# Query projection of the second layer in groups of four token tiles instead of two

## The chip, the core and the metric

One NeuronCore of a Trainium2 chip runs the whole program. The metric is the device time of one execution in microseconds (us). Its engines work side by side and wait for one another through semaphores: TensorE (PE; its weight loads are PEld), VectorE (DVE), ScalarE (ACT), GpSimd (POOL), and SyncE (SP), which here issues nearly all DMAs.

## The reference

Two kinds of layer alternate, twice each: A, B, A, B over 2048 tokens of width 576, with 32 heads of 18 channels.

```python
x = x + _A_ref(_layernorm(x), A_wq, A_wk, A_wv, A_wo)   # softmax attention, one key and value head
x = x + _B_ref(_layernorm(x), B_wqkv, B_w_phi, B_wo)    # linear attention on learned features
x = x + _A_ref(_layernorm(x), A_wq, A_wk, A_wv, A_wo)
x = x + _B_ref(_layernorm(x), B_wqkv, B_w_phi, B_wo)

def _A_ref(x, wq, wk, wv, wo):
    q = (x @ wq), split in 32 heads; k = x @ wk; v = x @ wv
    p = softmax(q k^T * 18 ** -0.5)
    return (p v, heads side by side) @ wo
```

What the change touches is `x @ wq`, `x @ wk` and `x @ wv` of the second A layer.

## The kernel before, in words

The program's "layer 0" is the first A and B pair, "layer 1" the second. Tokens lie in 16 tiles of 128. Each layer is (1) a setting up, which normalises every tile, turns it so that channels lie on partitions, and projects queries, keys and values; (2) a long attention part, in which ScalarE's exponentials and TensorE's score and value products alternate, with layer B's keys woven in; (3) a tail. The tail of layer 0's B layer and the setting up of layer 1 are one stretch: `token_tile` reads a tile's features back (`read_out`, L829), projects them with `wob` (L259), adds the residual (L324), and hands the tile on to `next_queries`.

**Ticks.** `pipelined` starts one tile per tick and moves every tile that is under way by one stage; jobs in `late` come at the end of the tick. So a tick of this stretch holds, from different tiles: the transposes of a normalised tile (`xn`, L310 and L314), the 28 products with `wob` on 288 columns, the transposes of a read-out (`xo`), and a read-out's 44 small products.

**Blocks.** After every second tile `next_queries` appends `project_queries` to `late`. Its core is 70 products, written together, which this text calls a block: five row tiles m (m = 4 first, which holds the last queries and the keys and values; its weights are `w4`), each the sum of 14 products over 256 columns (L467): four channel slots as high times high, high times low, low times high, and two products for the rest. The numbers are fp32 stored as an fp32r high part and the difference. For each m, ScalarE copies the bank to a piece `pc` (L492), VectorE makes the low part (L499) and a bf16 square (L501), and SP writes both parts to `qd` (L503). For m = 4 six further DMAs write the keys (L509), issued by SP, and by GpSimd for the last pair. After a STAGE, the next tick turns the values (L519), sums the squares over each head with `sel` (L523), and VectorE takes the maximum and a root (L524 to L529).

**Buffers.** The turned tokens lie in `xsc`, nine slots by 256 columns, with two buffers that alternate between pairs. `pc` has seven buffers. `featk` and `featq` are single buffers that lend `project_queries` its room. The seven banks of PSUM are handed out in turn.

**Order.** Instructions stand on each engine in the order that the scheduler gave them, and each engine runs in that order. `early` works beside the tiles: after four tiles it sets a level (`set_level`; L543 rewrites all of `kst`), after eight it loads the first queries and starts three score units.

Of the kernel before, what the change touches and what calls it, by code (L numbers as in the profile page):

```python
# [19 lines left out]
P = 128  # L20
S = 2048
D = 576
H = 32
DH = 18
NT = S // P
KT = 5
# [8 lines left out]
PAIR = 2  # L35
PW = PAIR * P
LEVEL = 4
KEYS = 3 * DH
STK = KEYS + 2
ROWT = 64  # L40
# [2 lines left out]
VROW = 64  # L43
# [19 lines left out]
def kernel(ctx, tc, x_in, wq, wk, wv, wo, wqkv, w_phi, wob, out):  # L63
    nc = tc.nc
# [242 lines left out]
    def transposed(xn, xs, ps, hi_engine, lo_engine=V):  # L307
        pa = ps.tile([P, 4, P], F32, name="ps")
        for k in range(4):
            T.transpose(pa[:, k, :], xn[:, k * P : (k + 1) * P], idf)  # L310
        split(xs[:, 0:4, :], xs[:, 5:9, :], pa, hi_engine, lo_engine)
        yield -440
        pb = ps.tile([P, P], F32, name="ps")
        T.transpose(pb, xn[:, 512:], idf)  # L314
        if hi_engine is A:
            A.activation(xs[:, 4, :], pb, AF.Copy)
        else:
            V.tensor_copy(xs[:, 4, :], pb)
        lo_engine.tensor_sub(xs[64:P, 4, :], pb[64:P, :], xs[64:P, 4, :].bitcast(F32))
        yield -110  # L320
# [127 lines left out]
    def clear_shifts():  # L448
        with tc.tile_pool(name="zero", bufs=1) as zp:
            z = zp.tile([P, 512], F32, name="z")  # L450
            V.memset(z, 0.0)
            for m in mxds:
                nc.sync.dma_start(m[1].rearrange("b c -> (b c)").rearrange("(p n) -> p n", p=P), z)

    def project_queries(p, layer, w, xsc, bw, pool, ps, norms):
        qd = qds[layer]
        keys = slice(p * PW, (p + 1) * PW)
        work = [bw.tile([P, H, 2, DH], F32, name=tag).rearrange("p h s d -> p (h s d)")
                for tag in ("featk", "featq")]
        sq = work[0][:, : KT * PW // 2].bitcast(BF16).rearrange("p (m t) -> p m t", t=PW)  # L460
        vt = work[0][:, KT * PW // 2 : KT * PW // 2 + PW]
        root = work[1][:H, :PW]

        def product(po, m, n):
            slot, half, k = PRODUCTS[n]
            lhs = w[half][:, k, m * P : (m + 1) * P] if m < 4 else w4[half][:, k, :]
            T.matmul(po, lhs, xsc[:, slot, :], start=(n == 0), stop=(n == LASTP))  # L467

        begun = {}
        opening = layer == 0 and p == 0  # L470
        if opening:
            for m in range(KT - 1):
                begun[m] = ps.tile([P, PW], F32, name="ps")
            mark = len(traced(nc))
            for n in range(len(PRODUCTS)):
                if n == TURN:
                    st["turn"]()
                for m in range(KT - 1):
                    product(begun[m], m, n)
        written_from = len(traced(nc))  # L480
        for m in (*range(KT - 1), KT - 1) if opening else (KT - 1, *range(KT - 1)):
            if layer == 0 and p == 1 and m == THIRD:
                st["turn third"]()
            po = begun.get(m)
            if po is None:
                po = ps.tile([P, PW], F32, name="ps")
                for n in range(len(PRODUCTS)):
                    product(po, m, n)
                if opening:
                    st["opening"] = traced(nc)[mark:]  # L490
            pc = pool.tile([P, 2, PW], F32R, name="pc", bufs=7)
            A.activation(pc[:, 0, :], po, AF.Copy)  # L492
            if m == 4:
                A.activation(vt, po, AF.Copy)
            top = pc[:, 0, :].bitcast(F32)
            squared = layer == 0 or p == NT // PAIR - 1
            if squared:
                A.activation(sq[:, m, :], po, AF.Square)
            V.tensor_sub(pc[:, 1, :], po, top)  # L499
            if not squared:  # L500
                V.tensor_mul(sq[:, m, :], top, top)  # L501
            rows = P if m < 4 else 64
            nc.sync.dma_start(qd[:, m * P : m * P + rows, keys].rearrange("j p t -> p j t"), pc[:rows].bitcast(F32))  # L503
            if m == KT - 1:
                queue = nc.gpsimd if p == NT // PAIR - 1 else nc.sync
                for j, piece in enumerate(KPIECES):
                    for base in (0, ROWT):
                        row = base + j * DH
                        queue.dma_start(kst[row : row + DH, keys].bitcast(F32),  # L509
                                          pc[KROW : KROW + DH, piece, :].bitcast(F32))  # L510
        if opening:
            st["third"]()
        elif layer == 0 and p <= 2:
            st["pinned"].extend(traced(nc)[written_from:])
        yield STAGE
        st["ready"] += PAIR
        pv = ps.tile([P, PAIR, P], F32, name="ps")
        for tt in range(PAIR):
            T.transpose(pv[:, tt, :], vt[:, tt * P : (tt + 1) * P], idf)  # L519
        V.tensor_copy(vst[:, p * PAIR : (p + 1) * PAIR, :DH], pv[:, :, VROW : VROW + DH])  # L520
        pn = ps.tile([P, PW], F32, name="ps")
        for m in range(KT):
            T.matmul(pn, sel[:, m, :], sq[:, m, :], start=(m == 0), stop=(m == KT - 1))  # L523
        V.tensor_reduce(norms[: H + 1, p : p + 1], pn[: H + 1], axis=AX.X, op=ALU.max)  # L524
        V.tensor_scalar(root.bitcast(I32), pn[:H].bitcast(I32), 1, None, op0=ALU.logical_shift_right)
        V.tensor_scalar(root.bitcast(I32), root.bitcast(I32), 1.0, float(0x1FC00000),
                        op0=ALU.mult, op1=ALU.add)
        length = pool.tile([P, PW], F32R, name="length", bufs=1)[:H]
        V.tensor_scalar(length, root, 1.02, None, op0=ALU.mult)  # L529
        nc.sync.dma_start(mxds[layer][0, :, keys], length.bitcast(F32))  # L530

# [314 lines left out]
            yield from project(po, st["wob"], b * HALF, xs, lambda: add_residual(i, b, po))  # L846

    def next_queries(i, stats, layer, st, xpool, sp, ps):
        p, tt = divmod(i, PAIR)
        xn = layer_norm(i, stats or ln_stats([i]), xpool, A)  # L850
        yield STAGE
        if tt == 0:
            st["xsc"] = sp.tile([P, 9, PW], F32R, name="xsc")
        xsc = st["xsc"]
        yield from transposed(xn, xsc[:, :, tt * P : (tt + 1) * P], ps, A)
        yield STAGE
        if tt == PAIR - 1:
            st["late"].append(project_queries(p, layer, st["wq"], xsc, bw, st["pieces"], ps, st["norms"]))

    def pipelined(jobs, late=(), fill=iter(())):  # L860
        jobs, active = deque(jobs), []
# [49 lines left out]
    def early(layer, st, ps):  # L911
        while st["ready"] < LEVEL:
            yield
        yield from set_level(st["norms"][:, : LEVEL // PAIR], st["limit"][layer], ps)
        while st["ready"] < BEGIN:
            yield
        for place in "ca"[: 1 if layer else 2]:
            st["head"] += room_spots(place)
            st["roomed"] += place
        load_queries(st["q0"], layer, 0, 0)  # L920
        load_shifts(st["q0"], layer, 0, 0)
        yield
        yield
        q1 = bw.tile([P, 9 * P], F32R, name="xs")
        st["q1"] = q1[:, : 2 * CW].rearrange("p (h t) -> p h t", t=CW)
        for n, pt in enumerate(st["head"]):
# [54 lines left out]
    def attend(layer, st, a1o, stream):  # L981
# [14 lines left out]
        with ctx1:  # L996
# [88 lines left out]
            last = {}  # L1085
# [47 lines left out]

            mark[0] = len(traced(nc))
            safe = []
            head(False, lambda: safe.append(decide_shift(st["norms"], st["limit"][layer], Spare())))
            in_order()
            last.clear()
            safe = safe[0]
# [181 lines left out]
    def settle(layer, ps, jobs):  # L1321
        st.update(ready=0, head=[], roomed="", begun=0)
        run(pipelined(jobs, st["late"], early(layer, st, ps)))
        st["slot"] = (ps.turn - 1) % 7 // 2 + 1

    with first, ExitStack() as ps:
        sp = s0
        st["pieces"] = s0q
        stats = {}

        def first_tile(i):
# [77 lines left out]
    for layer in range(LAYERS):  # L1409
# [196 lines left out]
        with psx, tc.tile_pool(name=f"s{layer + 1}", bufs=2) as sp, tc.tile_pool(name=f"s{layer + 1}q", bufs=1) as spq:  # L1606
            st["pieces"] = spq
            if not last:
                reload_w4(sp)

            def leave():
# [7 lines left out]
                both = sp.tile([P, 9, PW], F32R, name="xsc").bitcast(F32).rearrange("p a b -> p (a b)")  # L1619
                ek, eq = (both[:, k * 2 * D : (k + 1) * 2 * D].rearrange("p (h s d) -> p h s d", s=2, d=DH)  # L1620
                          for k in range(2))
# [88 lines left out]
```

## Time and profile before

| | us |
|---|---|
| median of three runs (2607.29, 2612.37, 2608.31) | 2608.31 |
| the profiled execution's own time | 2609.11 |
| its span, first to last instruction | 2607.2 |
| TensorE busy | 2576.6 |
| ScalarE busy | 2161.3 |
| VectorE busy | 1243.6 |
| setting up of layer 1, from its first block to its last products | 1253 to 1403 |

Times within the execution count from the start of the span. Busy time of TensorE is drawn from starts and modelled ends, and products overlap; so the price of a product is read from the distance between two starts of the timeline, not from its mean duration. The granted clock is 1.00 of full speed in every stretch used below.

### The profile page before, as it was taken

The page shows a single profiled execution, that of the slowest core. Times are in us where ns is not written, and L with a number is a line of the kernel's source. Part 1 is how long each engine was busy: PE and PEld are TensorE (multiplying, and loading weights), DVE is VectorE, ACT ScalarE, POOL GpSimd, SP SyncE. Part 2 cuts the span into 40 slices and gives each one's busy share as a digit, 9 for nine tenths or more (in the row PEclk, how much of TensorE's full clock was granted, in tenths as well). Part 3 has the DMA queues.
Part 4 walks back from the last instruction along what each step waited for, and adds up shares of the span by engine and source line. Part 5 has one row for each costly group of instructions (what it writes and reads, how often), then busy time and mean ns, then how long its engine had stood idle before and what let it go on. Part 6 is the DMA issues. An engine that isn't in the chain of part 4 may idle for free. (4 is left out here: it accounts for less than half of the span.)

```text
span 2607.2 us, 55668 instructions
## 1 busy us (share of the span) xinstructions
PE 2576.6 (99%) x22002; PEld 1429.5 (55%) x22002; DVE 1243.6 (48%) x2826; ACT 2161.3 (83%) x2583; POOL 89.0 (3%) x183
## 2 busy tenths in 40 slices
PE   8999999999999999999999999999999999999999
PEld 7634444444444444439996344444444444444598
DVE  7435554444444444427774424444444444444265
ACT  6699999999999999993336999999999999999721
POOL 1000000000000000002000000000000000000010
PEclk9999999999999999999999999999999999999999
DMA  6475442222222222226644312222222222222164
GB/s 201 142 179 146 120 138 61 60 54 56 58 60 57 58 58 61 61 53 189 200 129 148 80 44 61 61 59 56 61 57 61 61 61 61 61 61 59 35 200 144
DMA packets 491246, 232.96 MB, mean 89 GB/s; under 512 B 237902, under 2 KB 458166, under 8 KB 490978
## 3 DMA queue, kind: packets, MB, share of 16 engines
q1 hardware_dynamic: 490002, 227.04, 33.0%
q8 instruction: 176, 2.88, 0.5%
q0 software_dynamic: 976, 2.29, 0.3%
q14 instruction: 92, 0.75, 0.1%
HBM read 130.62 MB, written 96.67 MB: 87 GB/s over the span
## 5 line engine op out<-in xcount | busy, mean ns | idle before, releaser
L1103 ACT ACTIVATE pt<-sc 128x1024 f32<-128x1024 f32 x2032 | 1923.6, 1062 | 135.9 <-PE sc L598 114.9
L598 PE MATMUL sc<-qst,kst 56*128 56x512 f32 x3840 | 687.5, 450 | 1.5 <-ACT pt L1103 1.4
L598 PEld LDWEIGHTS sc<-qst,kst 56*128 56x128 f32 x3840 | 317.1, 184 | 555.3 <-ACT pt L1103 507.9
L878 PE MATMUL acc<-pt,vst 128*32 128x512 f32 x4096 | 510.7, 600 | 0.2 <-DVE vb L663 0.2
L878 PE MATMUL ps<-pt,vst 128*32 128x512 f32 x4048 | 481.3, 598 | 0.0
L878 PEld LDWEIGHTS ps<-pt,vst 128*32 128x32 f32 x4048 | 108.6, 109 | 224.4 <-issue 223.0
L878 PEld LDWEIGHTS acc<-pt,vst 128*32 128x32 f32 x4096 | 98.5, 108 | 200.7 <-issue 189.5
L324 DVE TENSOR_TENSOR xc<-xc,acc 128x288 f32<-128x288 f32 x59 | 26.8, 454 | 329.7 <-PE acc L259 329.7
L632 DVE COPY featq<-ps 128x288 f32<-128x288 f32 x52 | 23.8, 458 | 268.2 <-PE ps L259 268.2
L259 PE MATMUL ps<-wahi,xs 128*128 128x288 f32 x684 | 146.9, 301 | 0.6 <-ACT xs L133 0.6
L259 PE MATMUL ps<-wchi,xs 128*128 128x288 f32 x576 | 127.4, 306 | 0.0
L259 PE MATMUL acc<-wdhi,on 128*128 128x288 f32 x531 | 117.5, 306 | 0.0
L259 PEld LDWEIGHTS ps<-wahi,xs 128*128 128x128 f32 x684 | 111.8, 188 | 3.6 <-issue 1.7
L259 PE MATMUL ps<-walo,xs 128*128 128x288 f32 x380 | 111.3, 296 | 0.0
L467 PE MATMUL ps<-xsc,wbhi 128*128 128x256 f32 x576 | 109.1, 287 | 0.7 <-ACT xsc L133 0.6
L259 PE MATMUL acc<-wahi,xs 128*128 128x288 f32 x468 | 103.7, 307 | 2.4 <-DVE turned L1011 1.3
L291 POOL TENSOR_TENSOR rstd<-var,neghalf 128x1 f32<-128x1 f32 (+1 forms) x56 | 32.3, 576 | 2159.4 <-DVE mv L289 2142.2
L133 ACT ACTIVATE xs<-ps 128x512 fp32r<-128x512 f32 x36 | 21.4, 595 | 100.1 <-PE ps L310 100.1
L259 PEld LDWEIGHTS ps<-wchi,xs 128*128 128x128 f32 x576 | 94.1, 188 | 16.1 <-issue 15.8
L259 PEld LDWEIGHTS acc<-wdhi,on 128*128 128x128 f32 x531 | 86.5, 187 | 21.2 <-issue 21.2
L632 DVE COPY featk<-acc 128x288 f32<-128x288 f32 x52 | 23.8, 457 | 153.0 <-PE acc L259 153.0
L259 PE MATMUL ps<-wclo,xs 128*128 128x288 f32 x320 | 94.1, 294 | 0.0
(266 smaller groups left out, 3154.6 us busy)
## 6 DMA issues: line engine op xcount, KB each, us to landing
qst<-qd SPq DMA_DIRECT2D x360, 72.0 KB
od<-parts SPq DMA_DIRECT2D x512, 36.0 KB
pht<-phi SPq DMA_DIRECT2D x32, 540.0 KB
qd<-pc SPq DMA_DIRECT2D x64, 256.0 KB
on<-od SPq DMA_DIRECT2D x60, 256.0 KB
phi<-pht SPq DMA_DIRECT2D x104, 144.0 KB
xd<-xc SPq DMA_DIRECT2D x33, 288.0 KB
flipped<-pht SPq DMA_DIRECT2D x112, 72.0 KB
```

The source lines that it names most:

```text
L133: A.activation(dst_hi, src, AF.Copy)
L259: T.matmul(dst, xs[:, slot, :], w[half][:, k, c0 : c0 + HALF], start=(n == 0), stop=(n == last))
L291: G.tensor_tensor(rstd, var, neghalf[:, :n], op=ALU.pow)
L324: V.tensor_add(xr, xr, po)
L467: T.matmul(po, lhs, xsc[:, slot, :], start=(n == 0), stop=(n == LASTP))
L598: T.matmul(sc, kst[head_rows(h), t * P : (t + 1) * P], q[head_rows(h), h // 2, :], start=True, stop=True)
L632: V.tensor_copy(e[:, hs, 0, :], src)
L878: T.matmul(acc[32 * j : 32 * j + 32, :], vst[:, t, :], pts[j], start=first, stop=last)
L1103: A.activation(pt, sc, AF.Exp, scale=SCALE)
```

## The change

`GROUPS` gives each layer its groups of tiles: layer 0 keeps eight pairs, layer 1 has three groups of four and two pairs. A group of four is projected on 512 columns, one whole bank. The pieces `pc` of layer 1 become twice as wide and four instead of seven. `xsc` is one tile with two halves of two token tiles, in both layers; a group of four reads both halves at once. Of the group's room, the last square, the value rows and the root move to `featq`; the length is made in place. Layer 1's tail takes two `pc` buffers where it took one `xsc`.

```diff
+GROUPS = ((2,) * 8, (4, 4, 4, 2, 2))
+PIECES = (7, 4)
+    def piece_room(pool, layer):
+        widest = max(GROUPS[layer]) * P
+        return pool.tile([P, max(2 * widest, H * 2 * DH) if layer else 2 * widest], F32R, name="pc", bufs=PIECES[layer])
     def project_queries(p, layer, w, xsc, bw, pool, ps, norms):
-        keys = slice(p * PW, (p + 1) * PW)
+        size = GROUPS[layer][p]
+        width = size * P
+        begin = sum(GROUPS[layer][:p])
+        keys = slice(begin * P, (begin + size) * P)
+        tokens = xsc if size > PAIR else xsc[:, begin // PAIR % 2]
...
-            T.matmul(po, lhs, xsc[:, slot, :], start=(n == 0), stop=(n == LASTP))
+            moving = tokens[:, :, slot, :] if size > PAIR else tokens[:, slot, :]
+            T.matmul(po, lhs, moving, start=(n == 0), stop=(n == LASTP))
...
-                po = ps.tile([P, PW], F32, name="ps")
+                po = ps.tile([P, width], F32, name="ps")
...
-            pc = pool.tile([P, 2, PW], F32R, name="pc", bufs=7)
+            pc = piece_room(pool, layer)[:, : 2 * width].rearrange("p (j t) -> p j t", t=width)
...
     def next_queries(i, stats, layer, st, xpool, sp, ps):
-        p, tt = divmod(i, PAIR)
+        half, tt = i // PAIR % 2, i % PAIR
...
-        if tt == 0:
-            st["xsc"] = sp.tile([P, 9, PW], F32R, name="xsc")
...
-        yield from transposed(xn, xsc[:, :, tt * P : (tt + 1) * P], ps, A)
+        yield from transposed(xn, xsc[:, half, :, tt * P : (tt + 1) * P], ps, A)
...
-        if tt == PAIR - 1:
-            st["late"].append(project_queries(p, layer, st["wq"], xsc, bw, st["pieces"], ps, st["norms"]))
+        ends = [sum(GROUPS[layer][: p + 1]) - 1 for p in range(len(GROUPS[layer]))]
+        if i in ends:
+            st["late"].append(project_queries(ends.index(i), layer, st["wq"], xsc, bw, st["pieces"], ps, st["norms"]))
...
+    def token_room(pool):
+        return pool.tile([P, 2, 9, PW], F32R, name="xsc", bufs=1)
```

On all engines the instructions stand as before up to this stretch and after it; only names and widths differ. TensorE, where the first block stood before: behind the read-out of a tile came the first products on 256 columns (`w_14169` and `w_14170` are the two halves of `w4`, `kvb` and `pht` the read-out's operands).

```order
L310 MATMUL ps<-idf,xo 128x128 x4
L314 MATMUL ps<-idf,xo 128x128
L829 MATMUL ps<-kvb,pht 64x57 x20
L829 MATMUL ps<-kvb,pht 64x38 x2
L467 MATMUL ps<-xsc,w_14169 128x256
L467 MATMUL ps<-xsc,w_14170 128x256
```

In the changed kernel the same place on TensorE goes on with a further tile's transposes and its 28 products with `wob`.

```order
L312 MATMUL ps<-idf,xo 128x128 x4
L316 MATMUL ps<-idf,xo 128x128
L848 MATMUL ps<-kvb,pht 64x57 x20
L848 MATMUL ps<-kvb,pht 64x38 x2
L312 MATMUL ps<-idf,xn 128x128 x4
L316 MATMUL ps<-idf,xn 128x128
L261 MATMUL ps<-wahi,xs_15051 128x288
L261 MATMUL ps<-walo,xs_15051 128x288
```

The block has moved behind three more such ticks, to where the second pair's block stood, and holds both pairs; between the first and the second block, and between the second and the third, stand four ticks without one. Tile 4's transposes, too, stand ahead of the first block (tile 8's ahead of the second, tile 12's ahead of the third): they fill the quarter of `xsc` that the group's own first tile had, so that the products take the later tile's tokens there.

VectorE, one tick behind a pair's block, before: the values' copy, maximum and root (L520 to L529) among the steps of two other tiles.

```order
L520 COPY vst<-ps 128x2x18
L839 COPY xo<-xo 128x64
L524 TENSOR_REDUCE norms<-ps 33x1
L525 TENSOR_SCALAR featq<-ps 32x256
L136 TENSOR_TENSOR xsc<-ps,xsc 128x4x128
L526 TENSOR_SCALAR featq<-featq 32x256
L319 TENSOR_TENSOR xsc<-ps,xsc 64x128
L529 TENSOR_SCALAR length<-featq 32x256
L288 TENSOR_SCALAR var_15360<-mv_15355 128x1
```

VectorE at the same place behind the first group of four, after.

```order
L538 COPY vst<-ps 128x4x18
L858 COPY xo<-xo 128x64
L544 TENSOR_REDUCE norms<-ps 33x1
L545 TENSOR_SCALAR featq<-ps 32x512
L553 TENSOR_REDUCE top<-norms 33x1
L138 TENSOR_TENSOR xsc<-ps,xsc 128x4x128
L546 TENSOR_SCALAR featq<-featq 32x512
L321 TENSOR_TENSOR xsc<-ps,xsc 64x128
L548 TENSOR_SCALAR featq<-featq 32x512
L290 TENSOR_SCALAR var_15686<-mv_15681 128x1
```

The same steps stand there twice as wide, with `top` among them. Two further ticks without a block follow, where one did behind the first pair and none behind the others. VectorE two ticks later, after, where the level is written: `kst` (2048 columns) stands between the steps of two tiles.

```order
L579 TENSOR_TENSOR level<-ps,krows 128x1
L138 TENSOR_TENSOR xsc<-ps,xsc 128x4x128
L858 COPY xo<-xo 128x64
L562 TENSOR_SCALAR kst<-kst,krows,level 128x2048
L321 TENSOR_TENSOR xsc<-ps,xsc 64x128
L290 TENSOR_SCALAR var_15916<-mv_15911 128x1
```

Before, `kst` stood in the tick behind the third pair's norms, one tick ahead of a block; now it stands in the last tick ahead of the second block.

## Rows read from the trace of the kernel before

**Rows 1.** The page: busy time by engine, then the chain that ended last, by engine.

```profile
PE 2576.6 (99%) x22002; PEld 1429.5 (55%) x22002; DVE 1243.6 (48%) x2826; ACT 2161.3 (83%) x2583; POOL 89.0 (3%) x183
...
PE 45%; DVE 0%; ACT 0%; POOL 0%; issue 0%; DVEq 0%; POOLq 0%; ACTq 0%
```

**Rows 2.** Stretches of the second layer's setting up: length, busy (instructions) by engine, clock, DMA.

```profile
1253.02:1393.63 140.61, 140.58 (x1454) 136.11 (x1451) 100.82 (x320) 50.59 (x124) 9.93 (x26) 1.00 0.49 150
...
1253.02:1261.40 8.38, 8.38 (x74) 8.38 (x71) 4.91 (x18) 1.81 (x5) 0.93 (x2) 1.00 0.61 178
...
1268.50:1274.90 6.40, 6.40 (x85) 6.19 (x82) 5.84 (x20) 2.54 (x6) 0.73 (x2) 1.00 0.55 154
...
1274.90:1281.29 6.39, 6.39 (x87) 6.18 (x83) 5.67 (x19) 2.55 (x6) 0.73 (x2) 1.00 0.63 200
```

**Rows 3.** TensorE's timeline between blocks: start, length, line, names, number of instructions.

```profile
1267.76 0.44 PE L519 MATMUL ps<-idf,featk 128*128 128x128 f32 x2
...
1268.03 0.71 PE L523 MATMUL ps<-featk,sel 128*128 128x256 bf16 x5
...
1268.58 0.60 PE L310 MATMUL ps<-idf,xn 128*128 128x128 f32 x4
...
1269.04 0.38 PE L259 MATMUL ps<-wahi,xs 128*128 128x288 f32 x1
```

**Rows 4.** TensorE's timeline: two products of one tile's output, two of one block.

```profile
1341.99 0.29 PE L259 MATMUL ps<-walo,xs 128*128 128x288 f32 x1
...
1345.46 0.29 PE L259 MATMUL ps<-walo,xs 128*128 128x288 f32 x1
...
1349.52 0.28 PE L467 MATMUL ps<-xsc,wblo 128*128 128x256 f32 x1
...
1355.91 0.28 PE L467 MATMUL ps<-xsc,wblo 128*128 128x256 f32 x1
```

**Rows 5.** TensorE's timeline: one run of score products, cut after two, four and six.

```profile
188.68 0.49 PE L598 MATMUL sc<-qst,kst 56*128 56x512 f32 x2
...
188.68 0.72 PE L598 MATMUL sc<-qst,kst 56*128 56x512 f32 x4
...
188.68 0.96 PE L598 MATMUL sc<-qst,kst 56*128 56x512 f32 x6
```

**Rows 6.** VectorE by line, 1262 to 1393: names, shapes, count, busy us, mean ns, idle before.

```profile
L499 DVE TENSOR_TENSOR pc<-ps,pc 128x256 fp32r<-128x256 f32 x31 | 13.1, 424 | 20.4 <-ACT pc L492 20.3
...
L136 DVE TENSOR_TENSOR xsc<-ps,xsc 128x512 fp32r<-128x512 f32 x13 | 8.9, 682 | 1.5 <-ACT xsc L133 1.4
...
L524 DVE TENSOR_REDUCE norms<-ps 33x1 f32<-33x256 f32 x6 | 2.4, 406 | 0.0
...
L526 DVE TENSOR_SCALAR featq<-featq 32x256 int32<-32x256 int32 x6 | 1.6, 272 | 0.0
...
L543 DVE TENSOR_SCALAR kst<-kst,krows,level 128x2048 fp32r<-128x2048 f32 x1 | 1.3, 1328 | 0.0
```

**Rows 7.** VectorE's, then ScalarE's timeline ahead of a block; TensorE's first row of it.

```profile
1344.73 0.45 DVE L324 TENSOR_TENSOR xt<-xt,ps 128x288 f32<-128x288 f32 x1
...
1347.30 0.69 DVE L136 TENSOR_TENSOR xs<-ps,xs 128x512 fp32r<-128x512 f32 x1 [0.26 <-ACT xs L133]
...
1345.63 0.87 ACT L300 ACTIVATE xn<-xt,lnb,rstd 128x576 f32<-128x576 f32 x1 [2.91 <-POOL lnb L293]
...
1346.69 0.58 ACT L133 ACTIVATE xs<-ps 128x512 fp32r<-128x512 f32 x1
...
1347.63 1.93 PE L467 MATMUL ps<-xsc,w 128*128 128x256 f32 x14
```

**Rows 8.** Who issues DMAs from the pieces `pc`: ns min/median/max; then issue to landing.

```profile
L509 SPq DMA_DIRECT2D kst<-pc x84: 697/698/917, 30.9 to 1391.4; - x84
...
DMA to landing us min/median/max: 1.7/2.3/3.6
```

More of the change, by code (lines that the diff above doesn't have):

```diff
@@ L453, in clear_shifts @@
                 nc.sync.dma_start(m[1].rearrange("b c -> (b c)").rearrange("(p n) -> p n", p=P), z)
+    def piece_room(pool, layer):
+        widest = max(GROUPS[layer]) * P
+        return pool.tile([P, max(2 * widest, H * 2 * DH) if layer else 2 * widest], F32R, name="pc", bufs=PIECES[layer])
     def project_queries(p, layer, w, xsc, bw, pool, ps, norms):
         qd = qds[layer]
-        keys = slice(p * PW, (p + 1) * PW)
+        size = GROUPS[layer][p]
+        width = size * P
+        begin = sum(GROUPS[layer][:p])
+        tiles = slice(begin, begin + size)
+        keys = slice(begin * P, (begin + size) * P)
+        tokens = xsc if size > PAIR else xsc[:, begin // PAIR % 2]
         work = [bw.tile([P, H, 2, DH], F32, name=tag).rearrange("p h s d -> p (h s d)")
                 for tag in ("featk", "featq")]
-        sq = work[0][:, : KT * PW // 2].bitcast(BF16).rearrange("p (m t) -> p m t", t=PW)
-        vt = work[0][:, KT * PW // 2 : KT * PW // 2 + PW]
-        root = work[1][:H, :PW]
+        if size > PAIR:
+            rooms = [work[0][:, m * width // 2 : (m + 1) * width // 2] for m in range(KT - 1)]
+            rooms.append(work[1][:, : width // 2])
+            vt = work[1][:, width // 2 : width // 2 + width]
+        else:
+            rooms = [work[0][:, m * width // 2 : (m + 1) * width // 2] for m in range(KT)]
+            vt = work[0][:, KT * width // 2 : KT * width // 2 + width]
+        sq = [room.bitcast(BF16) for room in rooms]
         def product(po, m, n):
@@ L472, in project_queries @@
             for m in range(KT - 1):
-                begun[m] = ps.tile([P, PW], F32, name="ps")
+                begun[m] = ps.tile([P, width], F32, name="ps")
             mark = len(traced(nc))
@@ L495, in project_queries @@
             top = pc[:, 0, :].bitcast(F32)
-            squared = layer == 0 or p == NT // PAIR - 1
+            closing = p == len(GROUPS[layer]) - 1
+            squared = layer == 0 or closing
             if squared:
-                A.activation(sq[:, m, :], po, AF.Square)
+                A.activation(sq[m], po, AF.Square)
             V.tensor_sub(pc[:, 1, :], po, top)
             if not squared:
-                V.tensor_mul(sq[:, m, :], top, top)
+                V.tensor_mul(sq[m], top, top)
             rows = P if m < 4 else 64
@@ L504, in project_queries @@
             if m == KT - 1:
-                queue = nc.gpsimd if p == NT // PAIR - 1 else nc.sync
+                queue = nc.gpsimd if closing else nc.sync
                 for j, piece in enumerate(KPIECES):
@@ L515, in project_queries @@
         yield STAGE
-        st["ready"] += PAIR
-        pv = ps.tile([P, PAIR, P], F32, name="ps")
-        for tt in range(PAIR):
+        st["ready"] += size
+        pv = ps.tile([P, size, P], F32, name="ps")
+        for tt in range(size):
             T.transpose(pv[:, tt, :], vt[:, tt * P : (tt + 1) * P], idf)
-        V.tensor_copy(vst[:, p * PAIR : (p + 1) * PAIR, :DH], pv[:, :, VROW : VROW + DH])
-        pn = ps.tile([P, PW], F32, name="ps")
+        V.tensor_copy(vst[:, tiles, :DH], pv[:, :, VROW : VROW + DH])
+        pn = ps.tile([P, width], F32, name="ps")
         for m in range(KT):
-            T.matmul(pn, sel[:, m, :], sq[:, m, :], start=(m == 0), stop=(m == KT - 1))
+            T.matmul(pn, sel[:, m, :], sq[m], start=(m == 0), stop=(m == KT - 1))
+        root = work[1][:H, width // 2 : width // 2 + width] if size > PAIR else work[1][:H, :width]
+        length = pool.tile([P, PW], F32R, name="length", bufs=1)[:H] if layer == 0 else root.bitcast(F32R)
         V.tensor_reduce(norms[: H + 1, p : p + 1], pn[: H + 1], axis=AX.X, op=ALU.max)
@@ L527, in project_queries @@
                         op0=ALU.mult, op1=ALU.add)
-        length = pool.tile([P, PW], F32R, name="length", bufs=1)[:H]
         V.tensor_scalar(length, root, 1.02, None, op0=ALU.mult)
@@ L913, in early @@
             yield
-        yield from set_level(st["norms"][:, : LEVEL // PAIR], st["limit"][layer], ps)
+        level_groups = sum(1 for p in range(len(GROUPS[layer])) if sum(GROUPS[layer][:p]) < LEVEL)
+        yield from set_level(st["norms"][:, :level_groups], st["limit"][layer], ps)
         while st["ready"] < BEGIN:
@@ L1135, in attend @@
             safe = []
-            head(False, lambda: safe.append(decide_shift(st["norms"], st["limit"][layer], Spare())))
+            norms = st["norms"][:, : len(GROUPS[layer])]
+            head(False, lambda: safe.append(decide_shift(norms, st["limit"][layer], Spare())))
             in_order()
@@ L1328 @@
         st["pieces"] = s0q
+        st["xsc"] = token_room(s0)
         stats = {}
@@ L1608 @@
             if not last:
+                st["xsc"] = token_room(sp)
+            if not last:
                 reload_w4(sp)
@@ L1618, in leave @@
                 advance(queued[0])
-                both = sp.tile([P, 9, PW], F32R, name="xsc").bitcast(F32).rearrange("p a b -> p (a b)")
-                ek, eq = (both[:, k * 2 * D : (k + 1) * 2 * D].rearrange("p (h s d) -> p h s d", s=2, d=DH)
-                          for k in range(2))
+                if last:
+                    both = sp.tile([P, 9, PW], F32R, name="xsc").bitcast(F32).rearrange("p a b -> p (a b)")
+                    both = [both[:, k * 2 * D : (k + 1) * 2 * D] for k in range(2)]
+                else:
+                    both = [piece_room(spq, layer + 1).bitcast(F32) for _ in range(2)]
+                ek, eq = (room.rearrange("p (h s d) -> p h s d", s=2, d=DH) for room in both)
                 last_keys = keys_in(c, xl, ek, st, ps)
```

## The prediction

> **What bounds the kernel now.** I read the page first: TensorE is busy 99% of the span, and the chain that ended last runs over TensorE alone, the other engines at 0% [rows 1]. [...] A gain must come from products that take less time, and a loss from a wait that is not there yet. [...] In ticks without a block VectorE is busy 5.84 and 5.67 us of 6.40 and 6.39; within a block it is busy 4.91 of 8.38 [rows 2]. So the mean of VectorE (100.82 of 140.61, 72%) hides that it is nearly full (90%) in the ticks between blocks and rests in the blocks. The change puts longer runs of such ticks between longer blocks. These two facts make the sum.
>
> **The products.** Removed: 3 x 2 x 70 products on 256 columns. Added: 3 x 70 on 512. The columns streamed are the same, so the gain is whatever a product costs beside its columns. Between the two rows of one block lie 54 products in 1355.91 - 1349.52 = 6.39 us: 0.1183 each. Between the two rows of one tile's output lie 26 products on 288 columns in 1345.46 - 1341.99 = 3.47 us: 0.1335 each [rows 4]. Two of 256 cost 0.2367. What one of 512 costs, 128 rows deep, no row shows. I bound it:
> [...]
> - a straight line through 256 and 288 columns: 0.0152 us for 32 columns, so 0.1183 + 8 x 0.0152 = 0.2399. That is the upper end: 70 x 0.0032 = 0.22 us lost per group;
> - the nearest row in width: score products on 512 columns of the same type, 56 rows deep, two at a time on different rows of the array. The run ends at 0.49, 0.72 and 0.96 us after two, four and six of them, so a further pair costs 0.23 and 0.24 [rows 5]. I take the middle, 0.235, because the type and width are the same: 70 x 0.0017 = 0.12 us per group.
>
> The beginning and end of a block: 70 x 0.1183 = 8.28 us, while the block took 8.38 [rows 2]; the 0.10 is paid once instead of twice. Together 0.22 us per group, 0.7 us for three, between a loss of 0.4 and a gain of 2.8.
>
> [...]
>
> **Values and norms.** Behind a pair, two transposes and five bf16 products take 1268.58 - 1267.76 = 0.82 us on TensorE [rows 3]. [...]
>
> **ScalarE and VectorE within a block.** VectorE's low part takes 424 ns on 256 columns, a like operation 682 on 512 [rows 6]; so a group saves 10 x (2 x 424 - 682) = 1.7 us of VectorE's work. ScalarE saves as well. Neither gains a microsecond by itself: both lie beside a block of some 16 us. Cover gone, it would show as waiting behind the block, which the ticks' other work would have to do first.
>
> **The ticks between blocks.** Nothing is added to them in all, but their order is new. The norms come in the second tick behind a block. Before, a block came one tick later at most, and gave VectorE some 3.5 us of rest. Now two more ticks without a block follow. The norms are also wider: the maximum takes 406 ns on 256 columns; by the slope of the rows above (682 - 424 = 258 ns for 256 columns) it takes some 664, the shift as much, the two steps at 272 and some 280 ns perhaps 140 more each, the values' copy 40; with `top` (some 0.13) about 0.97 us more in that tick [rows 6]. How late may VectorE be there? In the shown tick VectorE ran late already (L324 started without a wait), ScalarE's `xn` waited 2.91 us for the statistics, the copy of `xs` stood behind it, and VectorE's low part of `xs` ended at 1347.30 + 0.69 = 1347.99 [rows 7]. A block hid that. With a tick in its place TensorE would want this low part after a tile's transposes (1269.04 - 1268.58 = 0.46 [rows 3]) and two products (0.27) behind 1347.63, at 1348.36: 0.37 us to spare. So 0.97 us more makes TensorE wait 0.97 - 0.37 = 0.6 us, in the third tick behind the first and behind the second group. In the fourth tick VectorE gets back 6.39 - 5.75 = 0.64 and pays about 0.56 for four small steps of the level, so nothing new. `kst` (1.33 us [rows 6]) falls just ahead of a block, which hides it. Behind the third group no read-out follows, and VectorE has time. So 1.2 us lost in all. Bounds: nothing, if the slack that the scheduler's order leaves is larger; and if VectorE ran without a gap and TensorE waited for all of it, three ticks of 5.75 with 2.5 of norms, 0.7 of the level and `kst` make 21.8 us against 19.2 behind the first group, 19.65 against 19.2 behind the second: 3.1 us.
>
> **Buffers and queues.** `xsc` is now single for a group, so the next tile's turned tokens may be written only when the block's last products have read it. That costs nothing, for the transposes that fill it stand behind the block on TensorE anyway. With four `pc`, the fifth piece of a group waits for the DMAs of the first. SP issues six key DMAs of 0.70 us and one to `qd`, so the first piece is issued some 1.5 + 5 us behind its products' end and lands 2.3 us later (3.6 at most) [rows 8]: about 3.3 + 10 = 13 us into the block; the fifth piece's products end at 16. Cover 3 us; if it is gone, the bank is held longer, and of seven banks two are free. SP has fewer DMAs, and the read-outs' loads still have two ticks, 12.7 us, as they have between the first two blocks now. All this at nothing.
>
> **The sum.** 2609.11 (the profiled execution) - 0.7 + 1.2 = 2609.6. The median of the runs shown lies 0.8 lower than that execution, so 2608.8. About 0.2%, 5.2 us here, is what a measurement of this kernel tells from no change.
>
> **The rivals.**
> [...]
> - *VectorE becomes the bound of the ticks* (the slower side). Its place is the ticks behind the first two groups; its price 3.1 us, with the products at their upper end 0.4 more: 2611.8. It decides if VectorE's work and its waits in a tick come to over 6.39 us; for it speaks 5.84 of 6.40. If a tick in a row of four costs 0.45 us each, then all twelve make 5.4 and the time passes 2613.5. Against it: two successive ticks of this kind passed with no wait of TensorE (1268.50 to 1281.29). Chance 0.17, of which 0.05 beyond 2613.5.
> - *Four pieces or SP's order hold the block up.* 1 us per group, 2611.8. Decides if the first piece's DMAs land over 16 us into the block. Chance 0.04.
> - *The change doesn't do what it says:* the three wide groups cost exactly twice a pair, and no wait comes. 2608.3; it can't be told from the forecast and is counted in it.
>
> **How the numbers follow.** Forecast: 0.54, from 2606.6 (0.230 a product, no wait) to 2611.1 (0.240 and twice the waits). Fixed cost 0.20, VectorE 0.17, pieces 0.04; what I don't see 0.05, to both sides. The range takes in the fixed cost's time and VectorE's, and the spread of the three runs: 2605.3 to 2612.6. Faster by over 0.2% needs more than the fixed cost gives: 0.04. Slower: 0.05 from VectorE and 0.02 from the rest: 0.07. Within: 0.89.
>
> **What would show it.** [...] TensorE's idle time over the stretch: 1.2 us, ended by VectorE's `xs` or ScalarE's `xn`, in the third tick behind the first two groups; nothing by DMAs. The stretch from the first products with `w4` to the score units should be within 1.5 us of its length before. Wrong would be: a wait for `pc`, for `pht`, or ticks of over 6.6 us in a row; or a block of under 15.5.

## The result and the profile after

The changed kernel takes 2613.99 us (median of 22 runs, 2610.11 to 2617.68), the kernel before 2609.18 us (22 runs beside it, 2606.62 to 2612.37): a ratio of 1.0017, 95% interval 1.0012 to 1.0023. It is slower by 4.8 us, about the size I had named as what can be told from no change, and 1.4 us past the upper end of my range. The profiled execution took 2611.43 us, with a span of 2609.7, against 2609.11 and 2607.2.

The page of the changed kernel, as [rows 1]: busy time by engine, the queue that brings TensorE its instructions (packets, MB, share), and the chain that ended last.

```profile
PE 2575.8 (99%) x21774; PEld 1416.7 (54%) x21777; DVE 1238.7 (47%) x2781; ACT 2158.0 (83%) x2565; POOL 88.5 (3%) x183
...
q8 instruction: 174, 2.85, 0.5%
...
PE 45%; ACT 0%; DVE 0%; issue 0%; POOL 0%; ACTq 0%; DVEq 0%; POOLq 0%
```

TensorE has 225 products less, 3 x 70 of the projections and 3 x 5 of the norms. The weight loads show it, 22002 before and 21777 now; the trace lists 228 products less, since three records of the norms' products are missing from it. TensorE is busy 0.8 us less, yet the span is 2.5 us longer. The page can't say where; it shows only that "issue" is now in the chain ahead of POOL. So I cut both traces at the same instructions. The first cut is the stretch from the first `xn` transposes of layer 1's tokens to the first score product of its attention. Columns: length, busy (instructions) of PE, PEld, DVE, ACT, POOL, granted clock, DMA share, GB/s. The kernel before:

```profile
1236.85:1402.54 165.69, 165.66 (x1751) 160.21 (x1749) 117.24 (x372) 61.96 (x157) 14.50 (x36) 1.00 0.53 161
```

The changed kernel: the stretch, its first wide block, and the tick in which the norms are done.

```profile
1236.17:1400.51 164.34, 164.15 (x1522) 148.17 (x1523) 113.13 (x327) 59.01 (x139) 14.06 (x36) 1.00 0.53 163
...
1271.50:1287.90 16.40, 16.40 (x75) 13.21 (x71) 7.11 (x18) 2.89 (x5) 0.73 (x2) 1.00 0.56 178
...
1294.30:1302.27 7.97, 7.92 (x92) 7.16 (x93) 7.27 (x24) 2.54 (x6) 0.73 (x2) 1.00 0.49 142
```

The change gains in the stretch that it touches: 165.69 - 164.34 = 1.35 us. No wait of TensorE is listed between the first block and the last one, and the block takes 16.40 us where twice a pair's took 16.76 [rows 2]. Inside it, two of TensorE's rows with 54 products between them (as [rows 4]: start, length, line, names, number):

```profile
1275.07 0.39 PE L484 MATMUL ps<-xsc,wblo 128*128 128x512 f32 x1
...
1287.67 0.39 PE L484 MATMUL ps<-xsc,wblo 128*128 128x512 f32 x1
```

(1287.67 - 1275.07) / 54 = 0.2333 us a product. Values and norms behind the block, as [rows 3], now take 1295.80 - 1294.22 = 1.58 us:

```profile
1294.22 0.66 PE L537 MATMUL ps<-idf,featq 128*128 128x128 f32 x4
...
1295.80 0.60 PE L312 MATMUL ps<-idf,xn 128*128 128x128 f32 x4
```

The loss comes behind the stretch, at the start of layer 1's attention, where every engine reads a value and jumps over the body of `tc.If` (L1140 before, L1160 now). TensorE's timeline there, before:

```profile
1409.08 0.91 PE L598 MATMUL sc<-wclo,kst 56*128 56x512 f32 x4
1411.00 0.69 PE L598 MATMUL sc<-wclo,kst 56*128 56x512 f32 x2 [1.01 <-ACTq L1140]
```

and in the changed kernel:

```profile
1407.05 0.91 PE L617 MATMUL sc<-wclo,kst 56*128 56x512 f32 x4
1408.87 0.46 PE L617 MATMUL sc<-wclo,kst 56*128 56x512 f32 x1 [0.91 <-ACTq L1160]
1411.55 0.47 PE L617 MATMUL sc<-wclo,kst 56*128 56x512 f32 x1 [2.21 <-issue]
```

Until 1408.87 the changed kernel leads by 2.1 us. Then TensorE stands still for 2.21 us between two score products that ran in one pair before, and the profile names no semaphore and no transfer for it. From the last four products ahead of the branch to the same score product some 150 matmuls later, the kernel before:

```profile
1409.08:1431.19 22.11, 21.10 (x147) 6.33 (x144) 10.61 (x18) 21.30 (x24) 0.00 (x0) 1.00 0.58 169
```

The changed kernel, and the part of it just behind the idle time:

```profile
1407.05:1433.14 26.09, 22.97 (x146) 6.70 (x142) 10.70 (x18) 21.39 (x24) 0.00 (x0) 0.93 0.55 154
...
1412.46:1415.20 2.74, 2.74 (x16) 0.44 (x8) 0.00 (x0) 0.61 (x1) 0.00 (x0) 0.50 0.58 133
```

3.98 us are lost here: 2.1 us of idle time, and 1.9 us because TensorE's busy time grew from 21.10 to 22.97 us for the same products, as its granted clock fell to 0.50 right behind the idle time. The whole difference of the two spans is then: 0.7 gained ahead of the stretch (1236.85 to 1236.17, where TensorE's instructions are the same in both; the granted clock was 0.57 from 22 to 26 us in the kernel before and 1.00 in the changed one, so this gain is not put down to the change), 1.35 gained in it, 3.98 lost at the branch, and 0.55 lost in all the rest (1176.01 us before, 1176.56 now), together 2.5.

### The profile page after: what moved, and what is told of

The parts are those of the page before. It is cut to its first block, busy times and chain, and to the rows that moved or that the text cites. A ratio compares the mean times of both kernels' runs of the same rounds, so it can differ in the third digit from the quotient of the medians.

```text
span 2609.7 us, 55057 instructions
## 1 busy us (share of the span) xinstructions
PE 2575.8 (99%) x21774; PEld 1416.7 (54%) x21777; DVE 1238.7 (47%) x2781; ACT 2158.0 (83%) x2565; POOL 88.5 (3%) x183
## 3 DMA queue, kind: packets, MB, share of 16 engines
q8 instruction: 174, 2.85, 0.5%
## 5 line engine op out<-in xcount | busy, mean ns | idle before, releaser
L484 PE MATMUL ps<-xsc,wbhi 128*128 128x256 f32 (+1 forms) x468 | 103.2, 313 | 0.7 <-ACT xsc L135 0.6
```

The lines of the kernel that those rows point to most:

```text
L484: T.matmul(po, lhs, moving, start=(n == 0), stop=(n == LASTP))
```

## The experiments

**Theory.** 225 products and 225 weight loads less ahead of the branch move all that follows in TensorE's program. TensorE's own queue of instructions brought 174 packets and 2.85 MB, 16 KB each; its program, counted as built, has 44,619 instructions (45,068 before, in 176 packets), so a packet is a block of some 256 instructions. If a block's edge falls just behind the target of a taken branch, TensorE waits for the next block. **Rival.** The wide projections themselves, or waits that they cause, cost the time.

The branch's body is never executed, so score products written there (dead products below) move the code behind them and add no work. To the changed kernel:

```diff
                 head(True)
+                if layer == 1:
+                    n = max(held)
+                    for _ in range(96):
+                        score(held[n][:, 1, :], st["q0"], 2 * units[n][2] + 1, units[n][1])
```

> The changed kernel with 96 score products (192 instructions of TensorE) written at the end of the branch body of layer 1's attention, which is never executed: no more work runs, but everything behind the branch stands 192 instructions later in TensorE's program, which puts the branch's target where the kernel before has it relative to blocks of 256 instructions (both at position 152 of such a block by count from the program's start; the changed kernel stands at 216). Theory (place of the code): the idle of 2.2 us ended by issue behind the first score product is gone, the granted clock stays at full speed around 1412 us, and the median is about 2608.6 (the kernel before less the 0.6 us that the second layer's projection stretch gives), that is 0.6 to 0.0 us under the kernel before. Rival (the projections themselves cost the time): idle or not, the median stays about 4.8 us above the kernel before, near 2614.

2613.74 us (ratio to the kernel before 1.0018, 1.0009 to 1.0027). The same with `range(32)` in the kernel before:

> The kernel before, its projections in pairs, with 32 never executed score products (64 instructions) in the same branch body, so that its branch target stands at position 216 of a block of 256 instructions, as in the changed kernel. Theory (place of the code): an idle of 2.0 to 2.6 us ended by issue appears behind the first or second score product, the granted clock falls to about 0.5 shortly behind it, and the median rises by 4 to 5.5 us, to about 2614. Rival (the projections cost the time): no change, 2609.2 within 1 us.

2613.98 us (1.0017, 1.0007 to 1.0026). `range(8)` in the changed kernel:

> The changed kernel with 8 never executed score products (16 instructions) in that body: the branch target stands at position 232 of a block, and the block's edge, which the changed kernel's trace puts 2 to 4 instructions behind its target, now lies before the target; the next edge is some 240 instructions away. Theory (place of the code): no idle by issue, median about 2608.6, as with 96. A variant of the theory by which any move costs: 2614. Rival (the projections cost the time): near 2614 as well, with no idle.

2613.80 us (1.0015, 1.0006 to 1.0024). `range(40)` in the kernel before:

> The kernel before with 40 never executed score products (80 instructions) in that body: target at position 232, past the edge. Theory (place of the code): as the kernel before, 2609.2 within 0.8 us, and no idle by issue; with 32 products 4 to 5.5 us more than with 40. Rival (the padding itself costs something, or the projections do): both padded forms of the kernel before read alike.

2614.26 us (1.0018, 1.0009 to 1.0027). The second run bears the theory out: the kernel before, not a product of its projections changed, takes the changed kernel's time. The other three do not fit it as I had put it, since all places were bad. What TensorE waited for (us, times, longest) tells them apart. Before with 32, the same stall as in the changed kernel:

```profile
PE sc L598 <- issue: 2.5, 1, 2.5
PE sc L598 <- ACTq L1140: 1.0, 1, 1.0
```

The changed kernel with 96 products: the stall is longer, and it comes in front of the target, not behind one product (the row of its timeline, then the stretch at the branch; with 8 products it is 4.1 us too).

```profile
1412.31 0.99 PE L617 MATMUL sc<-wclo,kst 56*128 56x512 f32 x2 [4.11 <-issue]
...
1407.28:1434.73 27.45, 23.34 (x148) 6.85 (x144) 10.61 (x18) 21.41 (x24) 0.00 (x0) 0.88 0.51 153
```

Before with 40:

```profile
PE sc L598 <- issue: 4.4, 1, 4.4
```

So the theory had to be sharpened: the target must be in the branch's own block or in the next one, and there not just ahead of its end. Padding inside the body had pushed it to the block after that. Padding in layer 0's body, which is some 22,000 instructions ahead, moves layer 1's branch and target together. That gives three sharper tests, with `score` repeated 48 times in the changed kernel, 12 and 56 times in the kernel before:

```diff
                 head(True)
+                n = max(held)
+                for _ in range((48, 0)[layer]):
+                    score(held[n][:, 1, :], st["q0"], 2 * units[n][2] + 1, units[n][1])
```

> The changed kernel with 48 score products (96 instructions of TensorE) in the branch body of layer 0, never executed, none in layer 1's: layer 1's branch and its target both stand 96 instructions later. The four runs before fit one picture: TensorE's instructions come in blocks of 256, and when the branch is taken only its own block and the next one are there. Counted with the edge where the traces put it, the branch of layer 1 stands at 132 in the kernel before and at 199 in the changed one, and the target some 307 behind it: at 185 of the next block before (71 instructions left), at 249 of it in the changed kernel (7 left, then the stall of 2.21 us), and two blocks on with 16 or 192 instructions more (stall of 4.10 us in front of the target). Here the branch stands at 39 and the target at 89 of the next block. Theory (block and place): no idle by issue at all, no clock drop behind the branch, median 2608.6 (2607.6 to 2609.2), 0 to 1.5 us under the kernel before. Rival (any added code or the projections cost the time): 2613.5 to 2614.5 again.

2606.71 us (0.9995, 0.9986 to 1.0004), 0.9 us below the range that I expected. The branch now costs TensorE no more than in the kernel before, and the stretch at it is the shortest of all; the projection stretch is what it was in the changed kernel:

```profile
PE sc L617 <- PEq L1160: 0.9, 1, 0.9
```

```profile
1234.37:1398.71 164.34, 164.15 (x1523) 148.16 (x1524) 113.10 (x327) 59.00 (x139) 14.06 (x36) 1.00 0.53 162
...
1406.56:1428.40 21.84, 20.93 (x148) 6.25 (x144) 10.78 (x18) 20.62 (x23) 0.00 (x0) 1.00 0.57 161
```

Just ahead of that stretch, however, the granted clock stood at the lower level without any stall:

```profile
1402.40:1405.60 3.20, 3.20 (x18) 0.80 (x20) 0.00 (x0) 2.67 (x4) 0.00 (x0) 0.50 0.03 11
```

From the first score product of layer 1 to that stretch it therefore took 7.85 us, where the kernel before and the changed kernel take 6.54. From the first score product to the end of the stretch it is 29.69 us here, 28.65 in the kernel before and 32.63 in the changed kernel: 2.94 us less than the latter, though both had the lower clock once.

> The kernel before with 12 never executed score products (24 instructions) in layer 0's branch body: layer 1's branch at 156, its target at 209 of the next block with 47 instructions left, whose 23 products take longer than a block's coming. Theory (block and place): nothing happens, 2609.2 within 0.8 us: dead code costs nothing by itself. Rival (any padded form of a kernel runs slower): 2613.5 to 2614.5, as the four padded forms so far.

2611.06 us (1.0007, 0.9998 to 1.0016). No stall; the median is 1.1 us outside what I expected. Its profiled execution, the slowest of the eleven (2612.92 us), has the lower clock level behind the branch without a stall:

```profile
PE sc L598 <- ACTq L1140: 1.0, 1, 1.0
```

```profile
1414.50:1417.50 3.00, 3.00 (x18) 0.72 (x8) 0.51 (x2) 1.47 (x2) 0.00 (x0) 0.50 0.80 252
```

> The kernel before with 56 never executed score products (112 instructions) in layer 0's branch body: layer 1's branch at 244, its target two blocks on. Theory (block and place): a stall by issue of 4.1 to 4.4 us in front of the target in layer 1, the median near 2614 (4 to 5.5 us up), and no stall in layer 0. Rival (dead code in layer 1's body, and not the place, was what cost): 2609.2, as in the control with 12.

2613.25 us (1.0015, 1.0006 to 1.0024), with the stall that the place foretold:

```profile
PE sc L598 <- issue: 4.3, 1, 4.3
```

All runs at the branch, counted in TensorE's program with 33 instructions ahead of its first one (that puts the edge where the changed kernel stalls). The stretch is that of the rows above, from the last four products ahead of the branch.

| kernel | branch at | target | left in its block | stall by issue, us | stretch at the branch, us | median, us |
|---|---|---|---|---|---|---|
| before | 132 | next block, 185 | 71 | none | 22.11 | 2609.18 |
| before, 12 in layer 0 | 156 | next, 209 | 47 | none | 23.68 | 2611.06 |
| changed, 48 in layer 0 | 39 | next, 89 | 167 | none | 21.84 | 2606.71 |
| changed | 199 | next, 249 | 7 | 2.2 | 26.09 | 2613.99 |
| before, 32 | 132 | next, 249 | 7 | 2.5 | 26.40 | 2613.98 |
| changed, 96 | 199 | two on, 185 | 71 | 4.1 | 27.45 | 2613.74 |
| changed, 8 | 199 | two on, 9 | 247 | 4.1 | 26.68 | 2613.80 |
| before, 40 | 132 | two on, 9 | 247 | 4.4 | 26.94 | 2614.26 |
| before, 56 in layer 0 | 244 | two on, 41 | 215 | 4.3 | 27.24 | 2613.25 |

Every form in the table with a stall has a median from 2613.25 to 2614.26, every form without one from 2606.71 to 2611.06. The rival has fallen as the cause of the loss. The four forms with the target two blocks on stood still 4.1 to 4.4 us, the two with it in the next block and 7 instructions left 2.2 and 2.5 us. That TensorE waits there for a block to come is my reading of these places; the traces show the idle time and name nothing that ended it but "issue".

**The parts of the change, by the stretch of the projections.** This stretch repeats from trace to trace (164.34 us in all four traces of the changed kernel in the table, 165.64 to 165.69 in the five of the kernel before), so single profiles tell here what medians can't. Three of the five runs below were executed once only (2610.96, 2606.41 and 2615.50 us, in the order shown). First the halves without groups of four:

```diff
-GROUPS = ((2,) * 8, (4, 4, 4, 2, 2))
+GROUPS = ((2,) * 8, (2,) * 8)
```

> The changed kernel with layer 1's tiles in eight pairs, as layer 0's: one token buffer in halves and four piece buffers, and no group of four. TensorE's instructions stand where they stand in the kernel before, to the instruction. Both theories on the loss agree here that it isn't in the halves: 2609.2 within 0.8 us, no stall by issue. What it tells: whether the buffer in halves and the fewer piece buffers alone cost or give anything; a wait of a tile's transposes on the previous pair's products would show as up to 8 waits of TensorE in the second layer's projection stretch and a median up to 2 us above.

2610.33 us (1.0003, 0.9994 to 1.0012), 0.3 us outside what I expected. In the stretch it loses 1.5 us, with one wait of TensorE; ahead of it ScalarE waited four times for a DMA from a piece to `kst` (the stretch, then the waits: us, times, longest).

```profile
1235.67:1402.83 167.16, 165.81 (x1750) 160.29 (x1748) 116.48 (x372) 61.22 (x157) 14.95 (x36) 1.00 0.53 160
```

```profile
ACT pc L509 <- DMA kst<-pc: 11.7, 4, 3.1
...
PE ps L484 <- ACT xsc L135: 1.3, 1, 1.3
```

Halves or fewer piece buffers? The kernel before with four of them in layer 1 and nothing else:

```diff
-            pc = pool.tile([P, 2, PW], F32R, name="pc", bufs=7)
+            pc = pool.tile([P, 2, PW], F32R, name="pc", bufs=7 if layer == 0 else 4)
```

> The kernel before with 4 piece buffers instead of 7 for layer 1's projections, all else as it is. The halves alone (with 4) took 167.17 us from the first transposes of layer 1's tokens to the first score product against 165.69 in the kernel before, 1.3 us of it one wait of TensorE on ScalarE's copy of the last tile's tokens, and ScalarE waited there 11.7 us in 4 waits for pieces on their way to HBM. Theory (the number of buffers is what costs): the same waits here, 166.8 to 167.3. Rival (the buffer in halves costs: a tile's copy waits for the products of the pair before last): 165.6 to 165.8 here, no such wait.

```profile
1235.04:1402.37 167.33, 165.97 (x1751) 160.29 (x1749) 116.53 (x372) 61.32 (x157) 14.98 (x36) 1.00 0.53 160
```

```profile
ACT pc L492 <- DMA kst<-pc: 12.0, 4, 3.1
...
PE ps L467 <- ACT xsc L133: 1.4, 1, 1.4
```

The same waits: the buffers cost it, not the halves. With groups of four, whose pieces come half as often, ScalarE waits only 0.5 us for such a DMA in the changed kernel, and TensorE not at all. Then VectorE's room, in the changed kernel with 48 dead products in layer 0 (4 here, 9 in the second run):

```diff
-        V.tensor_reduce(norms[: H + 1, p : p + 1], pn[: H + 1], axis=AX.X, op=ALU.max)
+        for _ in range(4 if size > PAIR else 1):
+            V.tensor_reduce(norms[: H + 1, p : p + 1], pn[: H + 1], axis=AX.X, op=ALU.max)
```

> The changed kernel as in the run with 48 dead products in layer 0 (no stall at the branch), with the 512-column reduction of each wide group's norms repeated 4 times instead of once: 3 more VectorE operations of 0.68 us, 2.0 us per wide group, 6.1 us in all. Read by the time from the first layer-norm transposes of the second layer's tokens to the first score product of its attention, 164.34 us in all traces of the changed kernel so far (165.65 in those of the kernel before), which repeat within 0.02. My prediction's step (VectorE's lateness behind a group reaches TensorE, 0.6 us per group, or 0 with little to spare): 2 us more of VectorE work should come through nearly whole, 4 to 6 us (168 to 170.4). Rival (VectorE has more than 2 us to spare behind a wide group, since its blocks leave it idle 2 us at a time): 164.3 within 0.3.

```profile
1235.13:1399.86 164.73, 164.63 (x1525) 148.20 (x1523) 116.90 (x336) 59.37 (x139) 14.07 (x36) 1.00 0.54 163
```

> The same with 9 reductions: 8 more of 0.68 us, 5.4 us per wide group, 16.3 us in all. My prediction's step: 14 to 16.3 us longer (178 to 180.7). Rival with 2 to 4 us to spare: 1.4 to 3.4 us per group come through (168.5 to 174.5). Rival with over 5.4 us to spare: 164.3 within 0.5, and then VectorE could not have become the bound here at any price the change could bring.

```profile
1235.45:1405.95 170.50, 167.30 (x1526) 149.01 (x1524) 125.82 (x351) 58.98 (x137) 14.07 (x36) 1.00 0.52 157
```

```profile
PE ps L312 <- DVE xo L858: 1.1, 2, 0.6
PE ps L312 <- ACT xn L302: 1.1, 2, 0.6
PE ps L261 <- DVE xs L138: 0.7, 2, 0.5
```

Of 2.0 us more per group, by the durations of the operations, 0.13 comes through, of 5.4 us 2.05. That is far from what my prediction's step would give, and near the rival. But two things limit the reading. Operations in a row overlap: VectorE's busy time in the stretch grew by 116.90 - 113.10 = 3.8 us and by 125.82 - 113.10 = 12.7, that is 1.3 and 4.2 us per group. And the scheduler changed VectorE's order: in the first group's norms' tick the tile's statistics (L287) start at 1298.02 us without the additions, and at 1304.53 in the first of these two runs, behind the other steps of that tick. So the runs show that 1.3 us more of VectorE's work per group need not reach TensorE; what the changed kernel's own order has to spare they don't measure. Last, groups of four throughout:

```diff
-GROUPS = ((2,) * 8, (4, 4, 4, 2, 2))
+GROUPS = ((2,) * 8, (4, 4, 4, 4))
```

> The changed kernel with four groups of four in layer 1 (no pairs) and the 48 dead products in layer 0; the branch's target lies in the next block with 63 instructions left, so no stall there is expected. By the products alone the fourth block gives what the others gave, 0.35 to 0.45 us (164.34 to about 163.9). Rival (the last group lies bare: its 16.4 us block starts one tile later, and ScalarE's copies and squares of 512 columns end later in front of the first scores): 165 to 167. Median 2606 to 2608 by the first, up to 2610 by the second.

2610.02 us (1.0003, 0.9994 to 1.0012). The rival's time holds: the stretch is 1.8 us longer than with two pairs at the end, though TensorE is busy less. Waits come up that are not there with the pairs:

```profile
1237.49:1403.65 166.16, 163.71 (x1450) 144.16 (x1448) 108.84 (x312) 59.40 (x133) 14.07 (x36) 1.00 0.53 161
```

```profile
PE ps L312 <- ACT xn L302: 1.9, 1, 1.9
PE ps L848 <- DMA pht<-phi: 1.4, 1, 1.4
PE ps L484 <- ACT xsc L135: 0.6, 1, 0.6
```

## Why the prediction was wrong

- **What bounds the stretch: right.** TensorE is busy 164.15 of 164.34 us in it.
- **The products: the mechanism right, the size too small.** 0.2333 us where I took 0.235, the score pairs' price. The three blocks took 16.40, 16.37 and 16.46 us, not 70 x 0.235 + 0.10 = 16.55: 1.05 us gained in all, not 0.66. No run shows the price of a product that stands behind the bound of 2.8 us gained and behind the 0.20 for the fixed cost; the runs showed 0.2333 us a product and 1.35 us gained in the stretch.
- **Values and norms:** 1.58 us, where twice a pair's 0.82 [rows 3] makes 1.64: another 0.18 us gained for three groups, for which the forecast has no term. With the blocks that is 1.23 of the 1.35 us measured.
- **The ticks between blocks: this step failed.** I forecast 1.2 us of waiting; there is none. The step set VectorE's added work against TensorE's tick as it was before, and left out that the same wider norms hold TensorE longer too. The rows behind the first group show it. VectorE last waited for TensorE here, before:

```profile
1338.64 0.45 DVE L324 TENSOR_TENSOR xt<-xt,ps 128x288 f32<-128x288 f32 x1 [0.91 <-PE ps L259]
```

and in the changed kernel, with the low part of `xs` in the norms' tick and TensorE's next transposes:

```profile
1292.38 0.45 DVE L326 TENSOR_TENSOR xt<-xt,ps 128x288 f32<-128x288 f32 x1 [0.45 <-PE ps L261]
...
1301.91 0.69 DVE L138 TENSOR_TENSOR xs<-ps,xs 128x512 fp32r<-128x512 f32 x1 [0.38 <-ACT xs L135]
...
1302.13 0.19 PE L558 MATMUL ps<-idf,top 33*1 33x33 f32 x1
...
1302.25 0.66 PE L312 MATMUL ps<-idf,xn 128*128 128x128 f32 x4
```

From that wait to the end of the low part it was 1347.99 - 1338.64 = 9.35 us before [rows 7] and is 1302.60 - 1292.38 = 10.22 now: 0.87 more, where I had 0.97. But TensorE, from the same point to where the next tile's transposes stand or would stand, took 1347.63 - 1338.64 = 8.99 us before and takes 1302.25 - 1292.38 = 9.87 now: 0.88 more, 1.58 - 0.82 = 0.76 of it by values and norms and 0.12 by the product with `top`. With the 0.46 and 0.27 us of my own working 0.38 us are left to spare, as the 0.37 before. In the norms' tick VectorE is busy 7.27 of 7.97 us, and nobody waits. The durations were right: the part `pc` on 512 columns takes 691 ns, the maximum 678 (I had 682 and 664):

```profile
L517 DVE TENSOR_TENSOR pc<-ps,pc 128x512 fp32r<-128x512 f32 x15 | 10.4, 691 | 23.6 <-ACT pc L509 23.6
...
L544 DVE TENSOR_REDUCE norms<-ps 33x1 f32<-33x512 f32 x3 | 2.0, 678 | 0.0
```

- **Buffers and queues: right for the change, for a reason that the runs make plain.** Four buffers are too few for pairs (1.6 us) and enough for groups of four.
- **The rivals.** VectorE as the bound of the ticks gave 2611.8, on the right side and for the wrong reason: its place shows no wait. Its price had the same gap: it set three of VectorE's ticks with the norms against 19.2 us, three ticks of TensorE without them, and these took 1308.65 - 1287.90 = 20.75 us (also, 17.25 + 2.5 makes 19.75, not 19.65).
- **What the prediction lacked, and what decides: the place of the code.** I had seen that the instructions stand as before ahead of the stretch and behind it, and from that took it that nothing could change there. The sum counted what 225 products cost, and nothing for where the rest of the program moves to. That is the missing term: 4.0 us in the profiled execution. Its 2.1 us of idle time come and go with the place; that the stall also brings the lower clock of the other 1.9 us is likely and not shown, since the lower level is found without a stall as well. Without it the same change is 0.8 us better than the kernel before by the cuts (1.35 gained, 0.55 lost in the rest), and 2.3 us by the medians, with an interval that includes no change.

Two things stay open. The 0.55 us in the rest of layer 1's attention and the end is not explained; it is also there with 48 dead products (1176.50 us) and not there with all fours (1176.03), so it isn't the wide products as such. And the cuts give 3.2 us of loss (3.98 + 0.55 - 1.35) where the medians differ by 4.8 (3.1 to 6.0 by the interval). The mean granted clock, which is on record for each execution, goes with that: the changed kernel's profiled execution is one of seven of its 22 at 0.999, whose mean is 2611.62 us, while the eight at 0.997 have 2615.14. Of all 77 executions of the forms with a stall 47 stand at 0.998 or lower, of 125 executions without one (81 of them of the kernel before) 12. Where in those executions the clock falls was not seen.

## What to carry to other kernels

A change that adds or removes instructions ahead of a taken branch moves the branch in its engine's program; by its place alone TensorE stood still 2.2 to 4.4 us here. Look at the first instructions behind each branch for idle time ended by "issue" before the change's own work is blamed or praised. A few never executed instructions in an earlier branch's body move it back and tell in one run whether the place is the cause. And where work grows on one engine, ask whether the same work also grows on the engine that waits for it, before the difference is put down as a wait.

## What the runs showed of the hardware

- In layer 1 TensorE stood still 0.9 to 1.1 us while the value was read and the branch taken, in the eight traces without a stall. With the target two blocks of 256 instructions on, by the count of the table, it stood still 4.1 to 4.4 us in all, and with the target in the next block and 7 instructions left a further 2.2 to 2.5 us behind the first product; with 47 left there was no stall.
- In the six traces with a stall the mean granted clock of the stretch at the branch was 0.87 to 0.94, in the kernel before 1.00. In the changed kernel it was 0.50 from 1412.46 to 1415.20 us, and TensorE's work in the stretch took 1.9 us longer, beside 2.1 of idle time. But it was 0.50 without a stall too: from 1402.40 to 1405.60 us with 48 dead products in layer 0, from 1414.50 to 1417.50 with 12. So the stall is not its only occasion; what else brings it wasn't tried.
- A weight load and product of this type on 512 columns, 128 rows deep, took 0.2333 us, on 256 columns 0.1183 and on 288 0.1335 [rows 4]: 512 columns cost 1.97 times 256.
